# Projection steps in two halves of 64 rows beside the score products, and two rounds to a period

## The chip, the cores and the metric

The kernel runs on one core of a Trainium2 chip. The number that counts is the device time of one execution in microseconds (us). The kernel before took 1330.79 us, the median of three runs (1327.95 to 1332.58). Five engines work side by side and wait for each other by semaphores: TensorE (PE; its weight loads are listed apart as PEld), VectorE (DVE), ScalarE (ACT), GpSimd (POOL) and SyncE (SP), whose queue issues most of the transfers (DMA).

## The reference

Four layers work on one sequence of 2048 tokens of 576 numbers: attention, a filter in the frequency domain, and both once more. The change lies in the two attention layers. There 32 heads of 18 numbers each attend to the last 256 tokens:

```python
H = 32; Dh = D // H; W = 256
qkv = (lambda x, *d: x.transpose(*d))((x @ wqkv).reshape(B, S, 3, H, Dh), 2, 0, 3, 1, 4)
q, k, v = qkv[0], qkv[1], qkv[2]
scores = jnp.einsum("bhqd,bhkd->bhqk", q, k) * (Dh ** -0.5)
mask = (idx[:, None] - idx[None, :] >= 0) & (idx[:, None] - idx[None, :] < W)
p = _softmax(jnp.where(mask[None, None], scores, -1e9), axis=-1)
o = jnp.einsum("bhqk,bhkd->bhqd", p, v)
x = x + (lambda x, *d: x.transpose(*d))(o, 0, 2, 1, 3).reshape(B, S, D) @ wo
```

Here x stands for the normalised input of the layer in the first line, and for the residual stream in the last.

## The kernel before, in words

Tokens are cut into 16 tiles of 128, heads into 8 groups of four. A **round** x is one head group and one tile, so a layer has 128 rounds (`NX`). Four products per round give the scores with the query on the output's rows (S, line 1172), four give them with the key there (E, line 1205). Two heads of a pair lie in rows 0 to 63 and two in rows 64 to 127 of the stacked q and k, so every S and E product uses one half of the array's rows, and products of different halves can be in flight together.

- From an S product VectorE takes the maximum of each query (`score_max`, line 1174). Four rounds' maxima are turned by TensorE (`m_rows`, tile tpm), copied by ScalarE (tile mt) and written into q as an additional row. This runs `LEAD` = 10 rounds ahead.
- From an E product ScalarE takes exponentials into a tile P (`exps`, line 1206); GpSimd zeroes what the mask excludes (lines 1208 and 1211).
- `part` (line 1225) multiplies P with the values; the sums of four rounds gather in one bank U. VectorE turns U (line 1230), GpSimd divides (line 1242), VectorE turns back (line 1246), and SP stores.
- **Projections**: q and k of later head groups come from 28 units of 128 output rows and 512 tokens. A unit is 14 matmuls of 128x512 (`proj`, line 1109; weights and inputs are split into a high and a low part) that add up in one bank. At its end ScalarE copies the bank out twice (lines 1121 and 1124), the first copy rounded, GpSimd subtracts the rounded one (line 1127), and SP writes both parts to memory, from where they are loaded in the stacked form. Five units are done in an opening stage (rounds -10 to -1), where only S products run beside them; 23 remain.

The stage that matters here is the mixed one: E rounds 0 to 117 (`MIX` = 118) beside S rounds 10 to 127 and the 23 units. Its order on every engine is the order in which the Python code issues instructions. `bursts` writes it in **thirds** of a period of four rounds: each issues one S, three E and two S products in a row, then either projection steps or value products (`part`). The tail after it (rounds 118 to 127) has no S products.

An accumulator bank of 128x512 floats is one of eight: S has three buffers, E three, pj (projection) one, U one. A matmul into a buffer waits until the reader of the product before it in that buffer has ended.

Of the kernel before, what the change touches and what calls it, by code (L numbers as in the profile page):

```python
# [8 lines left out]
F32 = mybir.dt.float32  # L9
# [6 lines left out]
S, D = 2048, 576  # L16
DF = 289
NF = 290
NT = 16
# [622 lines left out]
NQ = 8  # L642
# [223 lines left out]
def layer_a(tc, ident, eps, bp, big, src, dst, wqk_d, wv_d, wo_d, dc_d, gc_d, dram, copy, wvs, second, spectral, share):  # L866
# [17 lines left out]
    if True:  # L884
# [191 lines left out]
        with ExitStack() as c2:  # L1076
# [14 lines left out]
            def remainders():  # L1091
                while ended:
                    ended.pop(0)()

            def proj(i, c, bank=0):
# [5 lines left out]
                def mm(s, k):  # L1101
                    wk, p, xk = k
                    if s == 7 and c == 2 and 0 < i < 8:
# [5 lines left out]
                    T.matmul(box["ps"].rearrange("r (n p) -> r n p", n=NT) if second else box["ps"], w[:, wk], x, start=s == 0, stop=s == len(ks) - 1)  # L1109
                    if s == len(ks) - 1:  # L1110
# [6 lines left out]
                        by, rest = box["ps"], sg  # L1117
                        if second:
                            by = by.rearrange("r (n p) -> r p n", n=NT)
                            rest = sg.rearrange("r a (p n) -> r a p n", n=NT)  # L1120
                        A.copy(rest[:, 0], by)  # L1121
                        aside = 4 * i + c >= 14
                        if aside:
                            A.copy(rest[:, 1].bitcast(F32), by)

                        def remainder():
                            (P if aside else V).tensor_sub(sg[:, 1] if aside else rest[:, 1], sg[:, 1].bitcast(F32) if aside else by,  # L1127
                                                           (sg if aside else rest)[:, 0].bitcast(F32))
# [64 lines left out]
            def exps(x, pair, hp):  # L1193
# [9 lines left out]
                ps = pp.tile([128, 512], F32, name=f"E{x}_{hl_}", **(dict(tag="S", bufs=3) if pair and NX - LEAD <= x else dict(tag="E", bufs=3)))  # L1203
# [9 lines left out]

            us = {}
# [96 lines left out]
            def later(k, n, c):  # L1311
                for lag, f in zip(later.lags, (divide, back, store)):
                    steps.setdefault(k + lag, []).append((f, n, c))
                if c == 3:
                    for h in range(4):
                        steps.setdefault(k + (10 + 2 * h if n < NQ - 2 else 9 + h // 2), []).append((pack, n, h))

            later.lags = 1, 3, 4

            def lasting(p):  # L1320
                x, half = p
                i = x % NT
                return 0 if i == 0 else 216 if half else 432

            def source(p):
                x, half = p
                i = x % NT
                return x - 1 if half == 0 else x - 2 + 2 * (i % 2)
# [197 lines left out]
```

## Time and profile before

| what | us |
|---|---|
| median of three runs | 1330.79 |
| the profiled execution | 1330.75 |
| its span on the core | 1328.8 |
| TensorE busy in the span | 1294.7 |
| VectorE busy | 948.4 |
| ScalarE busy | 753.1 |
| GpSimd busy | 714.1 |
| first E product of each attention layer at | 127.9 and 806.4 |
| 472 S products (118 rounds) of the mixed stage in | 128.0 to 436.0 and 806.4 to 1115.8 |

Rows of the profile read: line, engine, operation, tile written <- tiles read, shape, and how often; then busy time and the mean of one in ns, and the idle time of the engine ahead of the group with what ended it. In a timeline the first number is the start in us and the second how long the row's instructions took together. A matmul's start is the time at which it was handed on, and its end is modelled. A weight load is a row of its own.

### The profile page before, as it was taken

The numbers are of one execution on the slowest core, as the hardware profiler recorded it, in microseconds if no ns is written. First come the engines' busy times: TensorE is split into PE (matmuls) and PEld (weight loads), VectorE is DVE, ScalarE is ACT, GpSimd is POOL, SyncE is SP. The second block draws the span as 40 slices with busy tenths as digits, with TensorE's granted clock in tenths as the row PEclk, the third lists the DMA queues.
The fourth block names the chain that finished last, engine by engine and source line by source line (L and its number), as shares of the span: only waits on it lengthen the run. The fifth ranks groups of instructions, "written<-read, shape, count | busy, mean of one in ns | idle before, by whom it ended". The sixth has DMA issues, their size and how long they took to land.

```text
span 1328.8 us, 33094 instructions
## 1 busy us (share of the span) xinstructions
PE 1294.7 (97%) x10911; PEld 956.4 (72%) x10911; DVE 948.4 (71%) x3136; ACT 753.1 (57%) x1896; POOL 714.1 (54%) x1200
## 2 busy tenths in 40 slices
PE   9999999999999999999999999999999999899998
PEld 8986666666665599975999975666666654798587
DVE  5417888888889587766674158888888887575855
ACT  5622776777767645543355325677766778574233
POOL 3258566776667443467221295567667667213821
PEclk9999999999999899999999999999999999999999
DMA  6857665765557737688873468566556658497874
GB/s 205 215 156 204 221 199 188 235 195 185 189 163 240 220 116 228 197 274 254 282 246 76 103 207 220 189 213 185 181 176 195 188 173 280 141 336 267 297 253 163
DMA packets 179487, 274.22 MB, mean 206 GB/s; under 512 B 67743, under 2 KB 77727, under 8 KB 177989
## 3 DMA queue, kind: packets, MB, share of 16 engines
q1 hardware_dynamic: 167007, 243.63, 58.5%
q0 software_dynamic: 4656, 13.44, 4.0%
q10 hardware_dynamic: 7654, 15.03, 3.3%
q8 instruction: 88, 1.44, 0.5%
q14 instruction: 82, 0.67, 0.2%
HBM read 164.54 MB, written 114.81 MB: 210 GB/s over the span
## 4 chain that ended last, share of the span: by engine, by line
PE 86%; DVE 5%; issue 3%; DMA 3%; ACT 2%; SPq 1%; POOL 0%; DVEq 0%; ACTq 0%; POOLq 0%
PE pj L1109 20%; PE S L1172 13%; PE U L1225 12%; PE vps L1005 9%; PE ops L802 6%; PE E L1205 6%; PE po L274 4%; PE pq L524 3%; PE p L503 2%; PE pf L274 2%; PE pi L600 2%; PE pz L312 1%; DVE jk L1174 1%; PE tpm L1185 1%; DVE us L1230 1%
## 5 line engine op out<-in xcount | busy, mean ns | idle before, releaser
L1174 DVE CUSTOM_DVE_ANT_0 jk<-S,mask 128x384 bf16<-128x384 f32 (+2 forms) x1024 | 488.5, 526 | 72.4 <-PE S L1172 38.0
L1206 ACT ACTIVATE P<-E 128x384 f32<-128x384 f32 (+2 forms) x1024 | 407.7, 479 | 171.0 <-PE E L1205 130.1
L1172 PE MATMUL S<-ks,qs 63*128 63x384 f32 (+2 forms) x1024 | 280.7, 374 | 3.5 <-DVE m L1174 1.3
L1208 POOL TENSOR_SCALAR_AFFINE_SELECT P<-P 128x512 f32<-128x512 f32 x256 | 163.3, 638 | 195.4 <-ACT P L1206 183.6
L1172 PEld LDWEIGHTS S<-ks,qs 63*128 63x128 f32 x1024 | 146.2, 184 | 117.8 <-DVE m L1174 89.3
L1205 PE MATMUL E<-qs,ks 64*128 64x384 f32 (+2 forms) x1024 | 222.2, 375 | 2.0 <-ACT P L1206 1.9
L1225 PE MATMUL U<-P,vq 128*19 128x128 f32 (+1 forms) x3840 | 190.7, 331 | 4.6 <-DVE us L1230 4.5
L1225 PEld LDWEIGHTS U<-P,vq 128*19 128x19 f32 x3840 | 96.6, 99 | 83.5 <-issue 20.3
L1109 PE MATMUL pj<-xh,wqh 128*128 128x512 f32 x360 | 155.4, 432 | 0.6 <-DVE sg L1127 0.4
L1211 POOL TENSOR_SCALAR_AFFINE_SELECT P<-P 128x512 f32<-128x512 f32 x224 | 143.2, 639 | 0.0
L1205 PEld LDWEIGHTS E<-qs,ks 64*128 64x128 f32 x1024 | 115.1, 186 | 16.3 <-ACT P L1206 10.0
L1109 PE MATMUL pj<-xh,wql 128*128 128x512 f32 x360 | 122.1, 415 | 0.0
L1109 PE MATMUL pj<-xl,wqh 128*128 128x512 f32 x288 | 119.6, 415 | 0.0
L802 PE MATMUL ops<-oroom 128*128 128x290 f32 (+1 forms) x812 | 114.0, 297 | 2.3 <-DVE ofree L848 1.2
L802 PEld LDWEIGHTS ops<-oroom 128*128 128x128 f32 x812 | 110.4, 189 | 2.9 <-ACT ofree L836 2.5
L1109 PEld LDWEIGHTS pj<-xh,wqh 128*128 128x128 f32 x360 | 67.6, 188 | 31.6 <-issue 13.8
L1174 DVE DVE_READ_ACCUMULATOR2_ANT m<- 128x1 f32 x1024 | 85.3, 83 | 0.0
L1121 ACT CAST sg<-pj 128x512 fp32r<-128x512 f32 x72 | 42.4, 589 | 73.2 <-PE pj L1109 65.1
L1109 PEld LDWEIGHTS pj<-xh,wql 128*128 128x128 f32 x360 | 64.2, 188 | 21.9 <-issue 10.8
L1230 DVE STREAM_TRANSPOSE us<-U 128x512 f32<-128x512 f32 x64 | 45.9, 716 | 30.6 <-PE U L1225 30.5
L1109 PEld LDWEIGHTS pj<-xl,wqh 128*128 128x128 f32 x288 | 54.2, 188 | 16.8 <-issue 9.0
L789 POOL TENSOR_TENSOR oroom<-oraw,oroom 64x128 fp32r<-64x128 f32 x26 | 14.0, 537 | 94.9 <-ACT oroom L787 44.4
(510 smaller groups left out, 2278.4 us busy)
## 6 DMA issues: line engine op xcount, KB each, us to landing
qk_d<-sg SPq DMA_DIRECT2D x56, 512.0 KB
qs<-qk_d SPq DMA_DIRECT2D x384, 72.0 KB
ks<-qk_d SPq DMA_DIRECT2D x348, 72.0 KB
op_d<-o SPq DMA_DIRECT2D x56, 256.0 KB
v_d<-vt SPq DMA_DIRECT2D x32, 304.0 KB
vq<-v_d SPq DMA_DIRECT2D x16, 608.0 KB
wt<-in_w SPq DMA_DIRECT2D x16, 580.0 KB
ofree<-x SPq DMA_DIRECT2D x16, 580.0 KB
```

The costliest lines, as they stand in the source:

```text
L274: T.matmul(ps[:, c, 0:NF], tail[r] if si == 4 else hl_(si), dcs[b // 2][r, b % 2], start=mi == si == 0, stop=si == 4)
L802: self.nc.tensor.matmul(self.ps[u][n][:, 0:self.n], x, self.w[p][:, (2 * wk + n) * self.n:(2 * wk + n + 1) * self.n], start=first and i == ...
L1005: T.matmul(ps[:, n, 0:288], xT(xk, c), w[:, wk, n * 288:(n + 1) * 288], start=i == 0, stop=i == len(ks) - 1)
L1109: T.matmul(box["ps"].rearrange("r (n p) -> r n p", n=NT) if second else box["ps"], w[:, wk], x, start=s == 0, stop=s == len(ks) - 1)
L1172: T.matmul(ps[:, 0:N], q[b:b + 63, pair, i * 128:i * 128 + 128], k[b:b + 63, pair, lo:hi], start=True, stop=True)
L1174: V.tensor_tensor_reduce(out=jk[:, 0:N], in0=ps[:, 0:N], in1=mask[:, 384 - N:384], scale=1.0, scalar=-3e38, op0=ALU.add, op1=ALU.max, accu ...
L1205: T.matmul(ps[:, 0:nq], k[b:b + 64, pair, j * 128:j * 128 + 128], q[b:b + 64, pair, j * 128:j * 128 + nq], start=True, stop=True)
L1206: A.activation(p[:, hl_, 0:nq], ps[:, 0:nq], AF.Exp, scale=SC)
L1208: P.affine_select(out=p[:, :, 0:128], in_=p[:, :, 0:128], pattern=[[0, 4], [1, 128]], compare_op=ALU.is_ge, fill=0.0, base=0, channel_mult ...
L1211: P.affine_select(out=p[:, :, 256:384], in_=p[:, :, 256:384], pattern=[[0, 4], [-1, 128]], compare_op=ALU.is_gt, fill=0.0, base=0, channel ...
L1225: T.matmul(U[32 * h:32 * h + 19, (q0 % 4) * 128:(q0 % 4) * 128 + 128 * (q1 - q0)], vts[n][:, j, h], pt[n, j][:, h, (q0 - j) * 128:(q1 - j) ...
L1230: V.transpose(u, U.rearrange("r (p n) -> r n p", n=NT))
```

## The change

Four things differ in the attention layers; names of lines below are those of the changed kernel where they differ.

1. In the mixed stage each projection step becomes two matmuls of 64 rows (lines 1115, tiles pj and pk): rows 0 to 63 of weights and inputs add up in the bank pj, rows 64 to 127 in a bank of their own, pk. That bank is taken from E, which has two buffers now.
2. At a unit's end ScalarE copies both banks out (line 1129), GpSimd adds them (`total`), ScalarE rounds the sum (`high`, line 1136), GpSimd subtracts (`remainder`), and SP sends. `total` is issued at the end of the period, the next two in the middle of the next one, the sending in the middle of the one after.
3. `mixed` replaces `bursts`. A period has two rounds, eight S and eight E products in turn, 59 periods in all. A step's halves stand between an S and an E product: rows 0 to 63 beside the product in rows 64 to 127 ahead of it, rows 64 to 127 beside the product behind it. The 23 units end in periods 1 to 48 with 14 steps in two periods (7 and 7), or in three (5, 5 and 4).
4. All value products of two rounds stand in one block at the period's end, behind which every second period has a `m_rows`. Its turned tile is always one of E's two buffers.

On TensorE, the steady state before: a burst of S and E products, five projection steps, and the next burst (S74_1_1 is a score product of round 74, E64_1 an exponent product of round 64, pj6_3 the unit's accumulator).

```order
L1172 MATMUL S74_1_1_4814<-ks0_1060,qs0_1058 128x384
L1205 MATMUL E64_1_4818<-qs0_1058,ks0_1060 128x384
L1205 MATMUL E64_3_4821<-qs0_1058,ks0_1060 128x384
L1205 MATMUL E65_0_4827<-qs0_1058,ks0_1060 128x384
L1172 MATMUL S75_0_1_4830<-ks0_1060,qs0_1058 128x384
L1172 MATMUL S74_1_0_4834<-ks0_1060,qs0_1058 128x384
L1109 MATMUL pj6_3_4804<-xl_110,wqh6_3628 128x512
L1109 MATMUL pj6_3_4804<-xh_109,wqh6_3628 128x512
L1109 MATMUL pj6_3_4804<-xl_110,wqh6_3628 128x512
L1109 MATMUL pj6_3_4804<-xh_109,wql6_3629 128x512 x2
L1172 MATMUL S75_0_0_4843<-ks0_1060,qs0_1058 128x384
```

The same engine now, the first half of a period of seven steps (pj4_2 and pk4_2 are the two half accumulators of one unit).

```order
L1187 MATMUL S30_0_1_2661<-ks1_1061,qs1_1059 128x384
L1219 MATMUL E20_0_2666<-qs1_1059,ks1_1061 128x384
L1187 MATMUL S30_1_1_2669<-ks1_1061,qs1_1059 128x384
L1115 MATMUL pj4_2_2673<-xh_109,wqh4_1895 128x512
L1115 MATMUL pk4_2_2675<-xh_109,wqh4_1895 128x512
L1219 MATMUL E20_1_2677<-qs1_1059,ks1_1061 128x384
L1219 MATMUL E20_2_2680<-qs1_1059,ks1_1061 128x384
L1115 MATMUL pj4_2_2673<-xl_110,wqh4_1895 128x512
L1115 MATMUL pk4_2_2675<-xl_110,wqh4_1895 128x512
L1187 MATMUL S30_0_0_2685<-ks1_1061,qs1_1059 128x384
L1219 MATMUL E20_3_2689<-qs1_1059,ks1_1061 128x384
```

Three E products stood together; now each stands between S products and halves of steps, and E20_2 takes the buffer of E20_0, E20_3 that of E20_1. The period's end on TensorE now:

```order
L1187 MATMUL S31_0_0_2730<-ks1_1061,qs1_1059 128x384
L1219 MATMUL E21_3_2734<-qs1_1059,ks1_1061 128x384
L1115 MATMUL pj4_2_2673<-xh_109,wqh4_1895 128x512
L1115 MATMUL pk4_2_2675<-xh_109,wqh4_1895 128x512
L1187 MATMUL S31_1_0_2741<-ks1_1061,qs1_1059 128x384
L1237 MATMUL U_1670<-P1_1_2498,vq1_1770 19x256 x4
L1237 MATMUL U_1670<-P1_0_2451,vq1_1770 19x128 x4
L1237 MATMUL U_1670<-P1_2_2563,vq1_1770 19x256 x4
L1237 MATMUL U_1670<-P1_3_2609,vq1_1770 19x128 x4
L1199 MATMUL tpm1_3_2763<-ident_76,m1_3_2558 16x128
```

The value products of rounds 18 and 19 stand in one block behind the last S product, and the turned maxima behind them. On ScalarE, around the end of unit pj4_2, now:

```order
L1220 ACTIVATE P1_7_2829<-E23_3_2851 128x384
L1129 COPY sg4_2_2858<-pj4_2_2673 128x512
L1129 COPY sg4_2_2858<-pk4_2_2675 128x512
L1220 ACTIVATE P1_8_2892<-E24_0_2893 128x384
L1220 ACTIVATE P1_8_2892<-E24_1_2904 128x384
L1220 ACTIVATE P1_8_2892<-E24_2_2907 128x384
L1220 ACTIVATE P1_8_2892<-E24_3_2916 128x384
L1136 CAST sg4_2_2858<-sg4_2_2858 128x512
L1220 ACTIVATE P1_9_2939<-E25_0_2940 128x384
```

The two copies stand behind the period's last exponential, and the rounding (CAST) stands between the two rounds of the next period, where before only a cast and a copy stood together.

The diff, cut to its core:

```diff
-                def mm(s, k):
+                def mm(s, k, half=None):
...
+                    r = slice(0, 128) if half is None else slice(64 * half, 64 * half + 64)
+                    opens, closes = half != 1, half != 0
...
-                    if s == 0:
-                        box["ps"] = pp.tile([128, 512], F32, tag="E" if bank else "pj", name=f"pj{i}_{c}", bufs=3 if bank else 1)
+                    if s == 0 and half is None:
+                        box["ps"] = pp.tile([128, 512], F32, tag="E" if bank else "pj", name=f"pj{i}_{c}", bufs=2 if bank else 1)
+                    elif s == 0:
+                        box[half] = pp.tile([128, 512], F32, tag=("pj", "pk")[half], name=f"{('pj', 'pk')[half]}{i}_{c}", bufs=1)
                     w = wt[i][0] if p == "h" else wt[i][1]
                     x = tokens(xT(xk, slice(0, S)), c) if second else xT(xk, cs)
-                    T.matmul(box["ps"].rearrange("r (n p) -> r n p", n=NT) if second else box["ps"], w[:, wk], x, start=s == 0, stop=s == len(ks) - 1)
-                    if s == len(ks) - 1:
+                    ps = box["ps" if half is None else half]
+                    T.matmul(ps.rearrange("r (n p) -> r n p", n=NT) if second else ps, w[r, wk], x[r], start=s == 0, stop=s == len(ks) - 1)
+                    if closes and s == len(ks) - 1:
...
-                        A.copy(rest[:, 0], by)
-                        aside = 4 * i + c >= 14
-                        if aside:
-                            A.copy(rest[:, 1].bitcast(F32), by)
...
+                        if half is None:
+                            A.copy(rest[:, 0], bys[0])
+                        else:
+                            for k, by in enumerate(bys):
+                                A.copy(rest[:, k].bitcast(F32), by)
+                        raw = sg.bitcast(F32)
+
+                        def total():
+                            P.tensor_add(raw[:, 1], raw[:, 0], raw[:, 1])
+
+                        def high():
+                            A.copy(sg[:, 0], raw[:, 1])
 
                         def remainder():
-                            (P if aside else V).tensor_sub(sg[:, 1] if aside else rest[:, 1], sg[:, 1].bitcast(F32) if aside else by,
-                                                           (sg if aside else rest)[:, 0].bitcast(F32))
-
+                            if half is None:
+                                V.tensor_sub(rest[:, 1], bys[0], rest[:, 0].bitcast(F32))
+                            else:
+                                P.tensor_sub(sg[:, 1], raw[:, 1], raw[:, 0])
+
+                        def send():
                             (nc.scalar if i < 2 else nc.sync).dma_start(qk_d[:, 128 * i:128 * i + 128, cs].rearrange("a r t -> r a t").bitcast(F32), sg.bitcast(F32))
-                        ended.append(remainder)
-                return [lambda s=s, k=k: mm(s, k) for s, k in enumerate(ks)]
+                        ended.append((remainder, send) if half is None else (total, high, remainder, send))
+                return [lambda half=None, s=s, k=k: mm(s, k, half) for s, k in enumerate(ks)]
...
-                tag = "E" if done < 70 else "S" if done < len(pj) else "pj"
-                return pp.tile([128, 4, 128], F32, tag=tag, name=name, bufs=1 if tag == "pj" else 3)
+                return pp.tile([128, 4, 128], F32, tag="E", name=name, bufs=2)
...
-                ps = pp.tile([128, 512], F32, name=f"E{x}_{hl_}", **(dict(tag="S", bufs=3) if pair and NX - LEAD <= x else dict(tag="E", bufs=3)))
+                ps = pp.tile([128, 512], F32, name=f"E{x}_{hl_}", **(dict(tag="S", bufs=3) if pair and NX - LEAD <= x else dict(tag="E", bufs=2)))
...
-            def bursts():
-
-                es = [(x, pair, hp) for x in range(MIX) for pair in range(2) for hp in range(2)]
-                ss = [(x + LEAD, pair, 1 - hp) for x, pair, hp in es]
...
+            us, U = {}, None
+
+            def sums():
+                nonlocal U
+                U = pp.tile([128, 512], F32, tag="U", name="U", bufs=1)
+                A.activation(U, eps.to_broadcast([128, 512]), AF.Copy, scale=0.0)
...
+            def mixed():
+                last = MIX // 2
+                ends = [1 + 47 * u // 22 for u in range(23)]
+                at, u = 70, 0
+                early, mid, end = {}, {}, {}
+                plan = lambda d, p, f, *a: d.setdefault(p, []).append((f, a))
...
+                for p in range(last):
+                    if u < 23 and p > ends[u]:
+                        u += 1
+                    want = 0 if u == 23 else -(-(70 + 14 * (u + 1) - at) // (ends[u] + 1 - p))
+                    some = []
+                    for x in (2 * p, 2 * p + 1):
+                        y = x + LEAD
+                        some += [(score_max, y, 0, 1), (exps, x, 0, 0), (score_max, y, 1, 1), (exps, x, 1, 0),
+                                 (exps, x, 0, 1), (score_max, y, 0, 0), (exps, x, 1, 1), (score_max, y, 1, 0)]
+                    for i, (f, *a) in enumerate(some):
+                        if i in (0, 8):
+                            loads(2 * p + i // 8)
+                        j = i // 2
+                        step = (j + 1) * want // 8 > j * want // 8
+                        if i % 2 and step:
+                            pj[at + n](1)
+                            n += 1
                         f(*a)
+                        if i % 2 == 0 and step:
+                            pj[at + n](0)
+                        if i == 7:
+                            behind(2 * p)
+                            run(mid, p)
...
+                    done += n
+                    for total, high, remainder, send in ended:
+                        total()
+                        for f in (high, remainder):
+                            plan(mid, p + 1, f)
+                        plan(mid, p + 2, send)
...
+                    for x in (2 * p - 2, 2 * p - 1):
+                        if x > 0 and x % NT:
+                            pv(x)
+                    if p % 2 == 0:
+                        m_rows(*divmod((2 * p + LEAD + 1) // 4, 4))
+                        if p:
+                            n, c = divmod((2 * p - 1) // 4, 4)
+                            plan(mid, p + 1, divide, n, c)
+                            plan(end, p + 1, back, n, c)
+                            plan(mid, p + 2, store, n, c)
+                            if c == 3:
+                                for h in range(4):
+                                    plan(early, p + 4 + h, pack, n, h)
...
-            U = pp.tile([128, 512], F32, tag="U", name="U", bufs=1)
-            V.memset(U, 0.0)
-            for f in bursts():
-                f()
...
+            mixed()
+            now = 0
```

More of the change, by code (lines that the diff above doesn't have):

```diff
@@ L1092, in remainders @@
                 while ended:
-                    ended.pop(0)()
+                    for f in ended.pop(0):
+                        f()
             def proj(i, c, bank=0):
@@ L1126, in remainder @@
[L1126 to L1128 removed]
+                        rest = sg.rearrange("r a (p n) -> r a p n", n=NT) if second else sg
+                        bys = [ps.rearrange("r (n p) -> r p n", n=NT) if second else ps for ps in ([box["ps"]] if half is None else [box[0], box[1]])]
@@ L1311, in later @@
             def later(k, n, c):
-                for lag, f in zip(later.lags, (divide, back, store)):
+                for lag, f in zip((1, 3, 4), (divide, back, store)):
                     steps.setdefault(k + lag, []).append((f, n, c))
[L1314 to L1323, printed above, removed]
@@ L1433, in layer_a @@
                 done += 1
-            U = pp.tile([128, 512], F32, tag="U", name="U", bufs=1)
-            V.memset(U, 0.0)
-            for f in bursts():
-                f()
-                done += 1
-            now = -(-4 * MIX // 3)
-            later.lags = 1, 3, 4
-            ahead = [(max(now, 2 * k - now), f) for k in sorted(steps) for f in steps.pop(k)]
-            for k, f in ahead:
-                steps.setdefault(k, []).append(f)
+            mixed()
+            now = 0
             for t in range(MIX, NX + 2):
```

87 lines of the change are left out of this document (20 added, 67 removed).

## The prediction

> **What bounds the kernel now.** I read the page's busy times first, then the chain that ended last, then busy times by stage, then the timeline of single instructions.
>
> ```profile
> PE 1294.7 (97%) x10911; PEld 956.4 (72%) x10911; DVE 948.4 (71%) x3136; ACT 753.1 (57%) x1896; POOL 714.1 (54%) x1200
> PE 86%; DVE 5%; issue 3%; DMA 3%; ACT 2%; SPq 1%; POOL 0%; DVEq 0%; ACTq 0%; POOLq 0%
> ```
>
> TensorE is busy for 97% of the span and is 86% of the chain, so a stage is worth what its TensorE time changes. The change touches the mixed stage of both attention layers. Busy times of PE, PEld, DVE, ACT and POOL there (first row), and the score products alone (line 1172, the other rows):
>
> ```profile
> 160.00:390.00 230.00, 229.31 (x2298) 141.03 (x2290) 197.62 (x763) 162.36 (x413) 156.89 (x235) 1.00 0.62 196
> 128.00:436.00 308.00, 133.68 (x472) 69.59 (x472) 1.00 0.64 203
> 160.00:390.00 230.00, 96.12 (x348) 50.28 (x348) 1.00 0.62 196
> 400.00:436.00 36.00, 20.04 (x61) 10.28 (x61) 1.00 0.79 258
> 806.40:1115.80 309.40, 133.71 (x472) 69.62 (x472) 1.00 0.65 196
> ```
>
> A round has four S products, so 472 are the 118 rounds: 308.0 us in the first layer and 309.4 in the second, together 617.4, or 5.23 us for two rounds, which will be one period. Where steps run (160 to 390), two rounds take 8 x 230 / 348 = 5.29 us; behind the last unit (400 to 436) 8 x 36 / 61 = 4.72. Per 5.29 us VectorE works 5.29 x 197.62 / 230 = 4.54, ScalarE 3.73 and GpSimd 3.61. TensorE's own work, from its timeline:
>
> ```profile
> 309.53 0.44 PE L1172 MATMUL S<-ks,qs 63*128 63x384 f32 x1
> 309.53 0.61 PE L1205 MATMUL E<-qs,ks 64*128 64x384 f32 x3
> 309.98 0.35 PE L1172 MATMUL S<-ks,qs 63*128 63x384 f32 x2
> 310.26 0.50 PE L1109 MATMUL pj<-xh,wqh 128*128 128x512 f32 x1
> 310.59 0.39 PE L1109 MATMUL pj<-xl,wqh 128*128 128x512 f32 x1
> 310.82 0.40 PE L1109 MATMUL pj<-xh,wqh 128*128 128x512 f32 x1
> 311.06 0.39 PE L1109 MATMUL pj<-xl,wqh 128*128 128x512 f32 x1
> 311.38 0.44 PE L1172 MATMUL S<-ks,qs 63*128 63x384 f32 x1
> 312.11 1.50 PE L1225 MATMUL U<-P,vq 128*19 128x256 f32 x32
> 313.54 0.44 PE L1172 MATMUL S<-ks,qs 63*128 63x384 f32 x1
> 309.81 0.19 PEld L1172 LDWEIGHTS S<-ks,qs 63*128 63x128 f32 x2
> ```
>
> Three pairs of one S and one E product, the two in different halves of the array, take 310.26 - 309.53 = 0.73 us. The second pair's work is handed on at 309.81 and the third pair's at 309.98: a pair costs 0.17 once they follow each other. Steps follow each other in 0.23 (310.59, 310.82, 311.06), but the first takes 0.33 and the last 0.32 up to the next S product: each change between half rows and full rows costs 0.09 to 0.10, and the first pair behind it 0.11 more for its exposed load. The value products of two rounds take 313.54 - 312.11 = 1.43. Before the change nobody waits for the exponentials:
>
> ```profile
> PEld S L1172 <- DVE m L1174: 30.0, 97, 0.4
> PEld E L1205 <- ACT P L1206: 1.2, 6, 0.2
> ```
>
> In these 230 us loads of E products waited for ScalarE for 1.2 us in all, with three buffers and at most three E products in a row.
>
> **The change part by part.** *TensorE's own work falls.* Per period and half of the array there are eight products of 0.17 and seven half steps of 0.23, or 2.97 us; with the value block (1.43) and a change of rows (0.10) 4.5 us, against 5.29. The halves stand in different rows, as S and E do, and two banks keep them apart; that they run together is not shown for them, only for S and E. [...]
>
> *E loses a buffer, and that sets the period.* The loop of one buffer, from rows of single instructions:
>
> ```profile
> 310.04 1.26 ACT L1206 ACTIVATE P<-E 128x384 f32<-128x384 f32 x3 [0.86 <-PE E L1205]
> L1206 ACT ACTIVATE P<-E 128x384 f32<-128x384 f32 x301 | 126.9, 497 | 52.6 <-PE E L1205 43.7 <-PE S L1172 8.7
> 306.55 0.89 ACT L1206 ACTIVATE P<-E 128x384 f32<-128x384 f32 x2
> 307.49 0.18 PEld L1205 LDWEIGHTS E<-qs,ks 64*128 64x128 f32 x1 [0.20 <-ACT P L1206]
> ```
>
> An E product handed on at 309.53 is read from 310.04: 0.51 us. The exponential lasts 0.49 to 0.50. Two that end at 306.55 + 0.89 = 307.44 let the waiting load start at 307.49: 0.05. So a buffer comes round in 0.51 + 0.49 + 0.05 = 1.05 us when TensorE waits for it, since the load itself waits and is exposed. With two buffers the third, fifth and seventh E product of a period each start at least 1.05 behind the one two places ahead: 3.15 us for six of the eight. TensorE takes its queue in order, so S products and halves behind a waiting E load wait too; the halves then fill no more than this wait. The first two products find their buffers free, since ScalarE empties both during the value block.
>
> The period of seven steps then: 3.15 to the seventh E product; 0.48 to the eighth, which goes by the sixth (that comes a step and a pair, 0.23 + 0.17, to 0.59 behind the fifth, the longer where its S product waits for VectorE); 0.60 to the value block (exposed load 0.10, half step 0.23, S product 0.17, change of rows 0.10); 1.43 for the block. Sum 5.66. Without steps 0.38 and 0.37 take the place of 0.48 and 0.60: 5.33.
>
> *Smaller terms*, from these rows:
>
> ```profile
> 306.21 0.85 PE L1225 MATMUL U<-P,vq 128*19 128x256 f32 x16
> 306.99 0.43 PE L1172 MATMUL S<-ks,qs 63*128 63x384 f32 x1
> 304.81 0.28 PE L1185 MATMUL tpm<-ident,m 128*16 128x128 f32 x1
> L1206 ACT ACTIVATE P<-E 128x256 f32<-128x256 f32 x24 | 7.9, 385 | 4.7 <-PE E L1205 4.7
> L1206 ACT ACTIVATE P<-E 128x128 f32<-128x128 f32 x24 | 5.4, 283 | 6.8 <-PE E L1205 4.2 <-PE S L1172 2.6
> L1124 ACT COPY sg<-pj 128x512 f32<-128x512 f32 x19 | 11.3, 596 | 0.0
> L1127 POOL TENSOR_TENSOR sg<-sg 128x512 fp32r<-128x512 f32 x19 | 24.5, 1287 | 0.1
> ```
>
> One period in eight has half the value block (0.78 instead of 1.43): -0.08 on average. One in eight has narrow E products, whose exponentials take 0.39 and 0.28: about -0.6 there, so -0.08. The turned maxima cost between 0.03 (hidden load) and 0.28 every second period and take an E buffer: +0.10. A unit's two copies (0.60 each) stand on ScalarE behind the last exponential and are hidden by the value block; if that cover were gone, the next E product would be read up to 1.2 late. The rounding, one more operation of 0.60 per unit, stands between the fourth and fifth exponential, when the fifth is about to be wanted: +0.3 per unit by my estimate (between 0 and 0.6), 23 x 0.3 / 49 = +0.14 a period. The new addition on GpSimd (1.29 as the subtraction) brings it to 3.61 + 23 x 1.29 / 49 = 4.2 of 5.7 us: hidden, as the block needs a tile P a period after its mask. The transfers of a unit leave about a period and a half later; the loads that want them are issued several rounds behind that by the same program, so I cost this at nothing.
>
> **Sum.** 49 periods with steps (a few have five or four; I let that go): 5.66 - 0.16 + 0.10 + 0.14 = 5.74, times 49 = 281. Ten without: 5.33 - 0.16 + 0.10 = 5.27, times 10 = 53. Together 334 us a layer against 308.0 and 309.4: +50.6. The profiled execution took 1330.75 us, 0.04 under the median, so 1381; I say 1380. The tail and the first projections have a buffer less too; there two of four E products per round use S's banks, and I take nothing.
>
> **Rivals.** *Faster: the loop doesn't bind.* If TensorE's and VectorE's work set the period, it lies between VectorE's 4.54 and today's 5.23; midway, 4.9, saves 0.33 x 118 = 39: 1292. For it speak TensorE's 97% and the changes of rows that fall away; against it that the loop would have to be under (4.9 - 1.43 - 0.60 - 0.48) / 3 = 0.80 us where three rows give 1.05. Below 0.91 (5.23 in place of 4.9) the change gains.
>
> *The load is not exposed.* If the load of a waiting E product went ahead of its wait, the loop is 0.10 shorter (a first S product lasts 0.44, later ones 0.34 to 0.35): 0.3 a period, 118 x 0.3 = 35, so 1345. [...]
>
> *The halves don't run together.* Then seven half steps more, 1.6 us, against an idle TensorE of 5.7 - 4.5 = 1.2: +0.4 for 98 periods, 1420.
>
> **How the numbers follow.** The forecast (1360 to 1400) has 0.52, the hidden load 0.14, serial halves 0.12, the faster rival 0.16, and something near no change between it and the hidden load 0.06. Within 0.3% (about 4 us) is what a measurement here can't tell from no change. So faster 0.16, same 0.06, slower 0.78. The range leaves out the lower part of the faster case and what lies above serial halves: 1310 to 1425; the forecast's own is 1350 to 1410.
>
> **What would show it.** Right: loads of E products waiting for ScalarE for tens of us per layer where it was 1.2; starts of every other E product 1.05 apart; VectorE under 80% in the stage; 472 S products in about 334 us. Wrong: that wait stays small; then the period is VectorE's (its share above 0.9) and the time falls. Halves that start in pairs 0.23 or more apart would show the last rival.

## Result: 7% slower, as forecast in kind, and almost twice as much as forecast in size

The changed kernel takes 1420.16 us, the median of four runs (1419.57 to 1426.9), against 1331.68 (1327.95 to 1335.38) before: a ratio of 1.0676, with a 95% interval from 1.0632 to 1.0720. That is 88.5 us more, where +50 was forecast; the time lies inside the range, near its upper end.

The profiled execution is the slowest of the four, 1426.9 us, with a span of 1425.2 against 1328.8. Its page, for the whole program: busy times, the shares of the chain that ended last, the clock granted to TensorE in 40 slices, and the two groups that hold the E products.

```profile
PE 1342.7 (94%) x11555; PEld 984.8 (69%) x11555; DVE 956.4 (67%) x3132; ACT 813.2 (57%) x1946; POOL 772.5 (54%) x1248
PE 73%; ACT 14%; DMA 6%; DVE 3%; issue 2%; SPq 1%; POOL 0%; ACTq 0%; DVEq 0%
PEclk9999999999987799999999999999999976999999
L1219 PE MATMUL E<-qs,ks 64*128 64x384 f32 (+2 forms) x1024 | 385.4, 403 | 54.2 <-ACT P L1220 50.5
L1219 PEld LDWEIGHTS E<-qs,ks 64*128 64x128 f32 x1024 | 188.9, 191 | 181.1 <-ACT P L1220 156.2
```

TensorE's share of the chain went from 86% to 73% and ScalarE's from 2% to 14%. E's loads and products now stand behind 156.2 and 50.5 us of idle time that the exponentials end. And the clock has two dips, in slices 12 to 14 and in slices 33 and 34.

**Where the time went.** The mixed stage of both layers: all its S products (first two rows), then the E products of its 49 periods with steps and of its last ten periods without, layer by layer. The last three columns are granted clock, DMA share and GB/s.

```profile
128.30:481.40 353.10, 153.98 (x472) 84.55 (x472) 0.94 0.58 181
857.30:1211.90 354.60, 154.14 (x472) 84.31 (x472) 0.94 0.57 174
128.30:412.40 284.10, 147.61 (x392) 71.87 (x392) 1.00 0.58 183
412.40:481.50 69.10, 35.52 (x81) 17.30 (x81) 0.70 0.55 173
857.30:1142.20 284.90, 147.46 (x393) 71.88 (x393) 1.00 0.57 175
1142.20:1211.90 69.70, 35.33 (x80) 16.95 (x80) 0.70 0.55 170
```

The stage takes 353.1 + 354.6 = 707.7 us instead of 617.4: +90.3 of the 96.2 by which the profiled executions differ. (Of the rest, 5.4 lie between the two stages: 857.3 - 481.5 = 375.8 against 806.4 - 436.0 = 370.4.) The two halves of the stage tell different stories:

| in one layer | before | forecast | measured |
|---|---|---|---|
| 49 periods with steps | 259.0 | 281 | 284.1 and 284.9 |
| 10 periods without | 49.1 | 53 | 69.1 and 69.7 |

The 259.0 and 49.1 are those of the kernel before for the same rounds. So the periods that the prediction worked on came out within 4 us; the ten short ones, to which it gave one line, hold 2 x 16 = 32 us that it didn't see.

**The loop that was forecast.** Waits between 180 and 400 us of the changed kernel (us in total, times, longest), and TensorE's timeline over part of one period with steps:

```profile
PEld E L1219 <- ACT P L1220: 46.5, 102, 0.7
PE E L1219 <- ACT P L1220: 15.1, 61, 0.5
PEld S L1187 <- DVE m L1189: 4.8, 26, 0.3
```

```profile
303.36 0.44 PE L1219 MATMUL E<-qs,ks 64*128 64x384 f32 x1
303.64 0.39 PE L1115 MATMUL pj<-xl,wqh 64*128 64x512 f32 x1
303.81 0.40 PE L1115 MATMUL pk<-xl,wqh 64*128 64x512 f32 x1
303.87 0.34 PE L1219 MATMUL E<-qs,ks 64*128 64x384 f32 x1
304.41 0.44 PE L1219 MATMUL E<-qs,ks 64*128 64x384 f32 x1 [0.20 <-ACT P L1220]
304.69 0.39 PE L1115 MATMUL pk<-xh,wql 64*128 64x512 f32 x1
304.92 0.34 PE L1219 MATMUL E<-qs,ks 64*128 64x384 f32 x1
304.93 0.39 PE L1115 MATMUL pj<-xh,wql 64*128 64x512 f32 x1
305.10 0.39 PE L1115 MATMUL pk<-xh,wql 64*128 64x512 f32 x1
305.16 0.33 PE L1187 MATMUL S<-ks,qs 63*128 63x384 f32 x1
305.33 0.39 PE L1115 MATMUL pj<-xh,wql 64*128 64x512 f32 x1
305.56 0.34 PE L1219 MATMUL E<-qs,ks 64*128 64x384 f32 x1
306.51 0.18 PEld L1219 LDWEIGHTS E<-qs,ks 64*128 64x128 f32 x1 [0.45 <-ACT P L1220]
```

The first four E products start at 303.36, 303.87, 304.41 and 304.92: the third and fourth each 1.05 behind the one two places ahead, the loop that was added up from three rows. Behind them it is not 1.05 each time. The fifth comes 1.15 behind the third: its load starts at 305.43, 1.02 behind, and its product 0.13 after that, while TensorE has halves of steps ahead of it. The seventh (its load and its product are both handed on at 306.51) comes 0.95 behind the fifth, whose own load was not the one that waited. From the first to the seventh that is 306.51 - 303.36 = 3.15 in this period; over the 49 periods of the first layer the middle value is 3.37 (counted from the starts of E products). Loads of E now wait 46.5 us for ScalarE in 220 us, where it was 1.2 in 230.

The two halves of a step start 303.81 - 303.64 = 0.17 apart, under the 0.23 of a whole step. In four of this period's seven steps they start 0.27 to 0.28 apart (the one at 304.69 is such a pk, whose pj started at 304.41), because rows 64 to 127 first take an E or S product. That the halves run together is seen in the whole step: with its S and E product it comes round in 305.33 - 304.93 = 0.40, which is 0.23 + 0.17; halves one behind the other would need 0.63.

**What was not forecast.** The last periods without steps, in stretches of about 3.4 us one behind the other (columns: sum of the stretch; PE, PEld, DVE, ACT and POOL busy; clock, DMA share, GB/s), then TensorE's timeline there:

```profile
432.50:435.95 3.45, 2.74 (x22) 1.36 (x14) 2.67 (x11) 2.40 (x6) 0.64 (x2) 0.99 0.82 243
436.00:439.40 3.40, 3.40 (x36) 1.57 (x36) 1.36 (x6) 1.13 (x3) 2.20 (x4) 0.50 0.15 55
439.45:442.75 3.30, 2.93 (x17) 1.67 (x13) 3.04 (x11) 2.44 (x7) 0.44 (x1) 1.00 0.24 71
```

```profile
433.81 0.44 PE L1219 MATMUL E<-qs,ks 64*128 64x384 f32 x1 [0.49 <-ACT P L1220]
434.83 0.44 PE L1219 MATMUL E<-qs,ks 64*128 64x384 f32 x1
435.85 0.61 PE L1219 MATMUL E<-qs,ks 64*128 64x384 f32 x1 [0.20 <-ACT P L1220]
436.85 2.71 PE L1237 MATMUL U<-P,vq 128*19 128x256 f32 x32
```

E's loop is still there (433.81, 434.83, 435.85: 1.02 apart). But in every second stretch from 425.7 us to 470.1 TensorE is granted half its clock (the rows show three stretches), and here the block of value products falls into it: it lasts 2.71 instead of the 1.43 to 1.50 of before. The kernel before does the same rounds (390 to 420 us) at a clock of 1.00. The waits of E's loads in this stage (415 to 481 us; us in total, times, longest) are short beside these stretches:

```profile
PEld E L1219 <- ACT P L1220: 15.8, 34, 0.9
```

### The profile page after: what moved, and what is told of

Read it like the earlier page. It is cut to its first block, busy times and chain, and to the rows that moved or that the text cites. A ratio compares the mean times of both kernels' runs of the same rounds, so it can differ in the third digit from the quotient of the medians.

```text
span 1425.2 us, 34356 instructions
## 1 busy us (share of the span) xinstructions
PE 1342.7 (94%) x11555; PEld 984.8 (69%) x11555; DVE 956.4 (67%) x3132; ACT 813.2 (57%) x1946; POOL 772.5 (54%) x1248
## 4 chain that ended last, share of the span: by engine, by line
PE 73%; ACT 14%; DMA 6%; DVE 3%; issue 2%; SPq 1%; POOL 0%; ACTq 0%; DVEq 0%
PE U L1237 13%; PE E L1219 11%; ACT P L1220 10%; PE vps L1005 8%; PE pj L1115 8%; PE ops L802 6%; PE S L1187 5%; PE pk L1115 4%; PE po L274 4%; PE pq L524 3%; PE p L503 2%; PE pf L274 2%; PE pi L600 2%; ACT sg L1136 2%; PE pz L312 1%
## 5 line engine op out<-in xcount | busy, mean ns | idle before, releaser
L1189 DVE CUSTOM_DVE_ANT_0 jk<-S,mask 128x384 bf16<-128x384 f32 (+2 forms) x1024 | 497.4, 524 | 105.7 <-PE S L1187 56.3
L1220 ACT ACTIVATE P<-E 128x384 f32<-128x384 f32 (+2 forms) x1024 | 442.2, 471 | 135.7 <-PE E L1219 69.1
L1219 PE MATMUL E<-qs,ks 64*128 64x384 f32 (+2 forms) x1024 | 385.4, 403 | 54.2 <-ACT P L1220 50.5
L1219 PEld LDWEIGHTS E<-qs,ks 64*128 64x128 f32 x1024 | 188.9, 191 | 181.1 <-ACT P L1220 156.2
L1115 PE MATMUL pj<-xh,wqh 64*128 64x512 f32 (+1 forms) x360 | 152.9, 425 | 0.0
L1115 PE MATMUL pj<-xh,wql 64*128 64x512 f32 (+1 forms) x360 | 142.2, 433 | 0.0
L1115 PE MATMUL pj<-xl,wqh 64*128 64x512 f32 (+1 forms) x288 | 125.6, 436 | 0.0
L1115 PE MATMUL pk<-xh,wqh 64*128 64x512 f32 x230 | 92.0, 400 | 0.0
L1115 PE MATMUL pk<-xh,wql 64*128 64x512 f32 x230 | 90.2, 396 | 0.0
L1115 PE MATMUL pk<-xl,wqh 64*128 64x512 f32 x184 | 73.2, 398 | 0.0
L1115 PEld LDWEIGHTS pj<-xh,wqh 64*128 64x128 f32 (+1 forms) x360 | 67.0, 186 | 7.1 <-issue 1.3
L1115 PEld LDWEIGHTS pj<-xh,wql 64*128 64x128 f32 (+1 forms) x360 | 66.9, 186 | 5.5
```

Of the source, the lines that this page charges most:

```text
L1115: T.matmul(ps.rearrange("r (n p) -> r n p", n=NT) if second else ps, w[r, wk], x[r], start=s == 0, stop=s == len(ks) - 1)
L1189: V.tensor_tensor_reduce(out=jk[:, 0:N], in0=ps[:, 0:N], in1=mask[:, 384 - N:384], scale=1.0, scalar=-3e38, op0=ALU.add, op1=ALU.max, accu ...
L1219: T.matmul(ps[:, 0:nq], k[b:b + 64, pair, j * 128:j * 128 + 128], q[b:b + 64, pair, j * 128:j * 128 + nq], start=True, stop=True)
L1220: A.activation(p[:, hl_, 0:nq], ps[:, 0:nq], AF.Exp, scale=SC)
```

## The experiments

The theory after the result: E's loop sets all periods, and in those without steps the waits it leaves cost the clock as well. Four questions follow. Is it the clock? Is the third buffer of E the missing thing? What is halving worth by itself? Which of the smaller terms was real?

### Filling the idle array: is it the clock?

In the ten periods without steps, seven pairs of half-row products (k with q, up to 384 columns) are added where the steps would stand, into the idle banks pj and pk. Nobody reads them; no work is left out.

```diff
                     some = []
+                    fill = 7 if u == 23 else 0
...
+                        idle = (j + 1) * fill // 8 > j * fill // 8
+                        if i % 2 and idle:
+                            again(2 * p + i // 8, 1)
...
+                        if i % 2 == 0 and idle:
+                            again(2 * p + i // 8, 0)
```

> The changed kernel with work added and none taken away: in the ten periods without projection steps, seven pairs of half-row products per period (an exponent product repeated into the idle banks pj and pk, read by nobody). Theory: those periods take 6.9 us instead of 5.3 because the granted clock falls to half when TensorE idles between E products; the added products fit into those waits, the clock in 415 to 480 us stays 1.00, the ten periods take 5.3 to 5.8 us each, and the time falls by 2 x 10 x 1.1 to 1.6 = 22 to 32 us, to 1388 to 1398. Rival (these periods are long for another reason, say the transfers or VectorE): added work can only cost, 1420 to 1440.

Measured: 1399.73 us (1398.32 to 1404.21), a ratio of 1.0525 (1.0503 to 1.0548), 2 us outside the expected range. More work makes the kernel 20 us faster. E products of the last ten periods in both layers, with the clock behind the counts:

```profile
414.00:472.10 58.10, 30.70 (x80) 14.64 (x80) 1.00 0.62 195
1130.50:1188.60 58.10, 30.72 (x81) 14.63 (x81) 1.00 0.65 196
```

The ten periods take 58.1 instead of 69.1 and 69.7 at a clock of 1.00 instead of 0.70: 22.6 us in the two layers, about the whole gain. So the clock it was, for at least this part. A period is then 5.8 long, the upper end of what I expected, as those with steps are.

The same with three pairs in place of seven (`fill = 3`), beside a new group of runs of the kernel before (median 1330.34):

> As the run with seven added pairs in the ten step-free periods, with three pairs per period. That run measured 58.1 us for the ten periods at a full clock, where the prediction's sum had 53. Theory: the clock goes by how long TensorE streams; if three pairs hold it, the periods cost less than with seven, 5.5 us each, and the time is 1390 to 1398; if they don't hold it, it lies between 1400 and 1420 with the clock between 0.70 and 1.00 in these periods. Rival (the clock has nothing to do with the added work): 1420.

Measured: 1407.22 (1405.43 to 1408.77), ratio 1.0580 (1.0563 to 1.0597), between the two, as expected for a clock that three pairs don't hold.

```profile
410.00:420.00 10.00, 9.18 (x88) 4.79 (x85) 8.12 (x31) 7.56 (x18) 7.24 (x10) 0.87 0.45 120
430.00:440.00 10.00, 9.06 (x105) 5.18 (x103) 7.72 (x29) 6.28 (x16) 5.07 (x10) 1.00 0.50 156
460.00:470.00 10.00, 8.72 (x60) 4.53 (x60) 8.95 (x31) 8.05 (x19) 5.84 (x9) 0.93 0.74 244
```

The clock is lost mostly at the start and at the end of the stretch. Over 410 to 460 us it is 0.97, against 0.73 with no pairs and 1.00 with seven: the more TensorE has to do there, the less of it is lost.

### The rounding on ScalarE moved: was the term of 0.14 real?

`high` and `remainder` go from between the rounds of the next period to its end, behind the last exponential.

```diff
-                            plan(mid, p + 1, f)
+                            plan(end, p + 1, f)
```

> The changed kernel with the rounding cast and the subtraction of a unit moved from the middle of the next period to its end, behind its last exponential, where the value block covers it. Theory: the cast of 0.6 us between the fourth and fifth exponential delays the fifth by about 0.3; without it 2 x 23 x 0.3 = 14 us less, 1406 (1398 to 1412). Rival (it stands in a gap of ScalarE anyway): 1420.

Measured: 1423.38 (1419.48 to 1427.00), ratio 1.0700 (1.0669 to 1.0731).

```profile
129.20:414.10 284.90, 148.44 (x393) 71.86 (x393) 1.00 0.58 182
```

The 49 periods take 284.9 as against 284.1: no gain. That does not make the term nothing, since the move covers the rounding in only some periods. In every second period the copy of the turned maxima (mt) comes ahead of it on ScalarE and waits for TensorE, so the rounding runs when the next period's first E product has already started (at 158.92), and its exponential stands behind both:

```profile
159.03 0.27 ACT L1201 ACTIVATE mt<-tpm 16x128 fp32r<-16x128 f32 x1 [1.39 <-PE tpm L1199]
159.20 0.61 ACT L1136 CAST sg<-sg 128x512 fp32r<-128x512 f32 x1
159.71 0.84 ACT L1220 ACTIVATE P<-E 128x384 f32<-128x384 f32 x2
```

Compared period by period in the first layer (starts of E products), fifteen roundings moved in this way: the periods that they left are 2.0 us shorter together, and those that they now open 3.9 longer. Seven others stand in periods without turned maxima and are covered (the 23rd falls behind the 49 periods): these are 1.0 shorter together, one of them like this (5.86 in the changed kernel, at 238.59 to 244.45):

```profile
240.60:246.14 5.54, 3.04 (x8) 1.46 (x8) 1.00 0.64 229
```

So a rounding between the exponentials did cost something, 3.0 / 22 = 0.14 a unit, about half of the 0.3 that I gave it, and this edit brought it back elsewhere. The other terms are seen in the changed kernel, in two periods that follow each other, the first with the turned maxima behind it and the second without:

```profile
198.66:204.70 6.04, 2.98 (x8) 1.47 (x8) 1.00 0.74 254
204.71:210.43 5.72, 3.10 (x8) 1.46 (x8) 1.00 0.51 159
```

Single periods differ, so here are means over the first layer: 5.83 for the twelve plain periods (5.51 to 6.20), 6.07 for the 25 with turned maxima, 5.36 for the six with narrow products and 5.04 for the six with half a value block. Spread over the 49, the turned maxima cost +0.12 where +0.10 stood, the narrow products save 0.06 where 0.08 stood, the half blocks 0.10 where 0.08 stood, and the rounding, which is part of these means, costs 22 x 0.14 / 49 = 0.06 where 0.14 stood. A plain period's 5.83 stands against 5.66 and the rounding's share.

### Two buffers for S in place of E: which bank is missing?

Every `bufs` of E goes from 2 to 3 and every one of S from 3 to 2 (one bank of the layer's output stage moves from S to E with them); the order stays.

```diff
-                return pp.tile([128, 4, 128], F32, tag="E", name=name, bufs=2)
+                return pp.tile([128, 4, 128], F32, tag="E", name=name, bufs=3)
...
-                ps = pp.tile([128, 512], F32, name=f"S{x}_{pair}_{hp}", bufs=1 if four else 3)
+                ps = pp.tile([128, 512], F32, name=f"S{x}_{pair}_{hp}", bufs=1 if four else 2)
```

> The changed kernel with three E buffers and two S buffers instead of two and three. Theory (the loop of a bank sets the period): the S loop is 0.51 + 0.55 + 0.08 + 0.05 = 1.19, longer than the 1.05 of E, so six of eight S products take 3 x 1.19 = 3.57 instead of 3.15: 0.4 per period, 118 x 0.4 = 50 more, about 1470 (1440 to 1490), and loads wait for VectorE where they waited for ScalarE. Rival (E's third buffer alone is what is missing): a period near 4.9, 1290 to 1330.

Measured: 1421.03 (1420.28 to 1421.77), ratio 1.0680 (1.0656 to 1.0703): both branches of the expectation are wrong. Waits between 180 and 400 us, and E products of the 49 and the last ten periods of the first layer:

```profile
PEld S L1187 <- DVE m L1189: 42.3, 150, 0.8
```

```profile
137.40:412.00 274.60, 123.30 (x392) 70.07 (x392) 1.00 0.59 187
412.00:483.10 71.10, 32.81 (x80) 16.78 (x80) 0.67 0.54 167
```

The wait moved from E's loads to S's (42.3 us, behind VectorE's maxima, where it was 4.8), and the loss stayed. So it isn't E's bank in particular: S takes the place of E as the loop. The periods are 274.6 / 49 = 5.60 long instead of 5.80, not the 6 and more that I expected: I had hung the tail of E's order on S's loop, though the last S product stands at the period's very end with only the change of rows and the block behind it. (Middle values over the 49 periods: 3.42 from the first to the seventh S product, where I had 3.57, then 0.42 to the eighth, and 1.76 from there to the next period.) The 0.2 saved per period (9.5 us in the first layer) is mostly lost ahead of them: the first E product comes at 137.4 instead of 128.3, behind an opening stage that runs S products, now with a buffer less (up to there their loads wait 9.5 us for VectorE, 2.2 in the changed kernel). Ahead of the second layer's stage 863.8 - 483.1 = 380.7 stands against 375.8, so 4.9 are lost there. The clock falls in the last ten here as well (0.67).

Both together, seven pairs of filling and three E buffers:

> Three E buffers and two S buffers with seven added pairs in the step-free periods. The run with three and two alone had 5.59 us per period with steps against 5.79, and lost 9 us in each opening stage. Theory (either bank pair sets a loop, and the clock is a cost of its own): the added pairs take about 11 us a layer off here too, 1421 - 22 = 1399 (1392 to 1406). Rival (the S loop leaves TensorE no room for added work): 1421 or more.

Measured: 1397.83 (1394.94 to 1398.64), ratio 1.0502 (1.0486 to 1.0518), as expected, and the least that any version with halves reached: still 5% over the kernel before.

### The kernel before with two buffers for E: the loop without the halves

One bank is left idle (the other uses of E's tag get two buffers as well); order and steps are those of before.

```diff
-                ps = pp.tile([128, 512], F32, name=f"E{x}_{hl_}", **(dict(tag="S", bufs=3) if pair and NX - LEAD <= x else dict(tag="E", bufs=3)))
+                ps = pp.tile([128, 512], F32, name=f"E{x}_{hl_}", **(dict(tag="S", bufs=3) if pair and NX - LEAD <= x else dict(tag="E", bufs=2)))
```

> The kernel before with two E buffers instead of three and nothing else. Theory: the third E product of each burst of three waits for the first one's buffer, 1.05 behind it instead of 0.45, 0.6 us in each of 157 bursts a layer: up to 188 us more, less where the burst waits anyway: 1450 to 1520. Rival (the buffer is not what the time hangs on): 1331 to 1345.

Measured: 1680.79 (1670.04 to 1691.55), ratio 1.2632 (1.2535 to 1.2729). TensorE's timeline over one burst, then all engines of the stage:

```profile
290.52 0.61 PE L1205 MATMUL E<-qs,ks 64*128 64x384 f32 x2
291.57 0.44 PE L1205 MATMUL E<-qs,ks 64*128 64x384 f32 x1 [0.44 <-ACT P L1206]
291.57 0.61 PE L1172 MATMUL S<-ks,qs 63*128 63x384 f32 x2
292.12 0.50 PE L1109 MATMUL pj<-xl,wqh 128*128 128x512 f32 x1
```

```profile
160.00:400.00 240.00, 200.23 (x1536) 108.44 (x1528) 139.83 (x510) 118.57 (x275) 105.98 (x159) 0.90 0.42 130
```

The third E product of a burst starts 291.57 - 290.52 = 1.05 behind the first: the same loop, in the old order, to the hundredth. Everything behind it waits too, two S products and then the steps, so a burst takes 292.12 - 290.52 = 1.60 instead of 0.73. There are 2 x 472 / 3 = 314 bursts: if all are like this one, that is 0.87 x 314 = 273 of the 349 us, an estimate. My expectation was too small, since it counted the wait of the third E product (0.6) and not that the S products come with it: from there to the first step it is 292.12 - 291.57 = 0.55, where it was 310.26 - 309.98 = 0.28. The clock of 0.90 (1.00 before) is in the rest; how much of the remaining 76 it makes was not separated. Against this the new order hides most of a wait that the old one can't.

### The new order with whole steps in one bank: what is halving worth?

Steps of 128 rows stand where the first halves stood, in the bank pj alone; E has its three buffers again. The unit's end has the cast and copy of the kernel before; its subtraction comes in the next period.

```diff
                         if i % 2 and step:
-                            pj[at + n](1)
                             n += 1
...
                         if i % 2 == 0 and step:
-                            pj[at + n](0)
+                            pj[at + n]()
...
+                return pp.tile([128, 4, 128], F32, tag="E", name=name, bufs=3)
```

> The order of the changed kernel with whole steps of 128 rows in one bank at the place of the first half, one copy less on ScalarE and no addition on GpSimd, and three E buffers. Theory: the loop no longer binds, but each step now stands between half-row products: 0.23 + 2 x 0.10 for the changes of rows + 0.11 for an exposed load on top of a pair's 0.17, seven times, one more pair 0.17 and the block 1.53: 6.7 us a period, 49 x 6.6 + 10 x 4.75 = 371 a layer against 308.7 before: 1331 + 124 = 1455 (1430 to 1480). The step-free periods come back to 4.7 to 4.9 at a full clock. Rival (the halves themselves cost the time, by their second bank's copies or by not running together): below 1420.

Measured: 1557.33 (1548.24 to 1566.42), ratio 1.1705 (1.1647 to 1.1762), 100 us more than expected. E products of the 49 periods, two successive steps in one of them, and the E products of four periods without steps:

```profile
127.70:499.80 372.10, 125.96 (x392) 54.91 (x392) 0.95 0.46 141
```

```profile
300.48 0.49 PE L1115 MATMUL pj<-xh,wqh 128*128 128x512 f32 x1
301.28 0.49 PE L1115 MATMUL pj<-xl,wqh 128*128 128x512 f32 x1
```

```profile
516.50:536.50 20.00, 10.44 (x32) 5.43 (x32) 1.00 0.69 201
```

A whole step alone among half-row products comes round in 0.80 with its pair of products, where a pair by itself takes 0.17 and a step among steps 0.23: two changes of rows and an exposed load at every step, which by the expectation's prices make 0.71; the other 0.09 was not traced. Periods take 372.1 / 49 = 7.6, part of it from the clock (0.95). Split in halves, and with a buffer less, the same order takes 5.80: in this order halving saves 1.8 us a period, the clock's part included. The last row bounds the price of the missing bank: four periods without steps, with three buffers for each of E and S, take 20.0, or 5.0 each at full clock, where I expected 4.7 to 4.9. With two for E they take 5.8 at full clock, but filled, so the bank costs at most 0.8 of a period there (an estimate, with the price of the filling in it), and 6.9 as the change leaves them. Only these four keep the clock: over the slices of 10 us from 500 to 560 it is 0.66 at both ends, and the ten periods take 56.3 (499.9 to 556.2). So this order loses the clock without steps even with three buffers; the missing bank is not the whole reason.

### The same filling in the kernel before: is there a better version?

The kernel before has a short dip of the clock in each layer (0.76 in 440 to 450 us, at the start of its tail, and 0.86 in 1110 to 1120). Products that nobody reads are added there and in the last rounds ahead of it.

```diff
+                    if k > 150:
+                        again(e[0][0])
...
+                    if t < MIX + 5:
+                        again(t)
```

> The kernel before with pairs of products added where its own clock falls (436 to 445 us and 1117 to 1121): after the bursts from third 151 on and twice a round in the first five rounds of the tail, in the idle bank. Theory: the tail of the run with seven added pairs took 16.6 us where before took 18.6 and 17.4; if the clock is held here, up to 3 us less, 1328. Rival (the waits there are VectorE's and ScalarE's, and added work stands behind them): 1331 to 1336.

Measured: 1330.64 (1329.02 to 1341.55), a ratio of 1.0009 (0.9992 to 1.0027). The mean clock of the profiled execution rises from 0.995 to 0.999, to 1.00 in both dips, and the time doesn't follow. Either these dips cost nothing or the added products cost what they return; the run doesn't tell which. No version here beats the kernel before.

## Why the prediction was right, and where its size failed

- **The bound was right, its form only in part.** The three-row sum of E's loop (1.05) is met to the hundredth where one waiting E product follows another, at the head of a period in the changed kernel and in the old order with two buffers. The 49 periods take 5.80 where 5.74 stood. But "3.15 to the seventh E product" is the least of it: the middle value is 3.37, as TensorE's queue adds 0.11 between the third and the fifth and a rounding lengthens the next gap. The close total owes something to the rounding, which cost less than its term. E's loads wait as described, and VectorE's share falls to 191.0 of 240 us, 80% (it was 86):

```profile
160.00:400.00 240.00, 222.63 (x2472) 139.08 (x2472) 191.00 (x727) 180.13 (x418) 177.19 (x248) 1.00 0.59 185
```

- **TensorE's own work did fall.** A step in halves comes round in 0.40 with its S and E product. The rival of serial halves is wrong, though its 1420 is the time that came and its sign (halves 0.23 or more apart) is met in four of seven steps: a number that fits is no proof of its mechanism. The faster rival needed a loop under 0.91, which it isn't. The hidden load would have shown 0.95 each time and 2.85 to the seventh product; 0.95 is seen, but only in the one place a period where the load ahead was not the one that waited.
- **That the time lies in the range is luck in part.** The forecast's own range was 1350 to 1410, which 1420 is outside of; the stated range reached up to 1425 only to take in the serial halves, which are not what happened.
- **The step that failed is the second line of the sum**, "Ten without: 5.33 - 0.16 + 0.10 = 5.27, times 10 = 53". It measured 69.1 and 69.7. The sum has no term for the clock: it goes by prices from rows of before, where the clock is 1.00, and here it is 0.70; with seven pairs of filling it is 1.00, so TensorE had too little work to keep it. Filling returns 11.0 and 11.6 us of the 16 to 17 per layer; what the added products cost is in that, so the clock's share is at least this much. The other 5.1 (58.1 against 53) is at full clock; by the prediction's own terms a filled period is longer by (0.48 - 0.38) + (0.60 - 0.37) = 0.33, ten of them by 3.3, and 1.8 is left. How long these periods are at full clock without filling was not seen.
- **Smaller terms**: the rounding cost 0.06 where +0.14 stood, and the turned maxima (+0.12), the narrow products (-0.06) and the half blocks (-0.10) each came within 0.02 of their terms. Against this the plain period is about 0.1 longer than its 5.66. Together they leave 0.06 (5.80 against 5.74).
- **Left out altogether**: 5.4 us between the two layers' stages in the profiled execution, where the prediction said "I take nothing". In the run with seven pairs of filling the same stretch is 845.5 - 472.1 = 373.4, so 2.4 of the 5.4 went with the dip ahead of it; the other 3.0 have no experiment.

The two layers' ten periods (69.1 + 69.7 - 106 = 32.8), the 49 (284.1 + 284.9 - 562 = 7.0) and the 5.4 make 45.2 of the 45.6 by which the profiled executions differ beyond the forecast 50.6. The median lies 6.7 below the profiled execution.

## What to carry to other kernels

An accumulator bank is a turn in a loop: add up product to reader, the reader's time and release to the next load from single rows, divide by the number of buffers, and compare it with the time per product, before a bank is traded for anything. This sum is the least; what stands in the engine's queue between the release and the load comes on top (1.16 instead of 1.05 in the middle of a period here). Taking it from the neighbour moved the loop here, as the exchange of E's and S's third buffers showed (S's loads then waited 42.3 us for VectorE where it was 4.8). And where a change makes TensorE wait, its clock can be one more term of the sum (0.70 in the ten periods here, 1.00 once filled): look at the parts of the stage with the least work, and test by adding work that nobody reads.

## What was not expected of the hardware

- Half the clock with short waits: E's loads wait at most 0.9 us in the periods without steps, and from 425.7 us to 470.1 the clock alternates between 1.00 and 0.50 in stretches of 3.4 us. Of a period's own time, products of the two halves of the array fill about 8 x 0.17 + 1.43 = 2.8 us, an estimate from rows of before. That is 2.8 / 4.72 = 59% in the kernel before and 56% in the 5.0-us periods with whole steps, where four periods in a row keep the clock, and 53% of the 5.27 us forecast, where it is lost. These lie too near each other to name a limit, and the periods with whole steps lose it too, ahead of those four and behind them; that more work on TensorE holds the clock is shown by the filling (0.70 without it, 1.00 with seven pairs), where between the two it tips is not.
- Adding 140 pairs of products that nobody reads (7 x 10 in each layer) made a kernel 20 us faster.
- The same loop of 1.05 costs 0.5 us per two rounds in one order (5.80 against 5.29, with what the halves save already taken off) and 0.87 per burst in another, of which two rounds hold 8 / 3, or 2.3 us. In the second, two S products and the steps stand in TensorE's queue behind the waiting load.
